# Sparse attention and FFN on one core: one written order for all engines, q and k ahead of the weights, and products of zeros at the beginning

## The chip, the cores and the metric

The kernel runs on one core of a Trainium2 chip. The metric is the time of one execution on the device in microseconds (us). A core has five engines that work side by side and wait for each other by semaphores: TensorE (PE in the profile; PEld is its weight load) multiplies matrices into PSUM; VectorE (DVE) and ScalarE (ACT) work element by element and can read PSUM; GpSimd (POOL) works element by element on SBUF; SyncE (SP) only issues transfers here. The kernels before and after are compared by the medians of their runs; the profile shows one execution.

## The reference

Eight batches, eight heads, 576 positions, heads of 64. Four heads look back over 32 positions, four at the positions of the same class modulo 32. The result, 4608 rows of 512, goes through a feed-forward layer with a gate that is 0 below -1, h above 1, and (h+1)^2/4 between.

```python
scores = scale * np.matmul(q, k.transpose(0, 1, 3, 2))
mask_local = (rel >= 0) & (rel < stride)
mask_strided = (rel >= 0) & (pos[None, :] % stride == pos[:, None] % stride)
...
scores = np.where(masks[None, :, :, :], scores, -1000000000.0)
scores = scores - np.max(scores, axis=-1, keepdims=True)
attn = np.exp(scores)
attn = attn / (np.sum(attn, axis=-1, keepdims=True) + 1e-09)
return np.matmul(attn, v).astype(np.float32)
...
x = np.ascontiguousarray(attn_out.transpose(0, 2, 1, 3)).reshape(B * S, H * D)
...
h = x @ w_in
g = np.where(pos, h, np.where(neg, 0.0, (h + beta) ** 2 / (4.0 * beta)))
return (g @ w_out).astype(np.float32)
```

## The kernel before, in words

**The feed-forward part.** The 4608 rows are cut into 12 chunks of 512, 384, 256 and then 384 rows. For each chunk c a loop runs over the 16 blocks f of 128 hidden units. `up(c, f)` makes the hidden block `hp` in PSUM with 12 products: four 128-wide pieces of x, each as three products of high and low parts (x and the weights are kept as two numbers each, so that the fast fp32r products are exact enough). The gate follows: ScalarE's Relu (L372) and Square (L373), VectorE's max and min (L374), then `gh`, the high part (L376 on ScalarE, L378 on VectorE in chunk 0), and `gl`, the low part (L379 on VectorE). `down(c, f)` adds three products for each 128 rows of the chunk into the output sums, 12 in chunk 0 and 9 in a chunk of 384. It runs two blocks behind `up` (`LAG = 2`). `hp` has two buffers in PSUM, so `up` of block f+2 waits until `gl` of block f has been read out.

**The weights.** Each f has 1 MB of float64 words (w_in's block and w_out's block side by side). They are loaded once, by SP, and turned to float32 pairs on the chip (`convert_w`): ScalarE's Prelu (L174) and Copy (L176) on the two words, VectorE's shift (L180), GpSimd's add (L181), then ScalarE's cast to the high part (L186) and VectorE's subtract for the low part (L188). One weight has two halves, so each step comes twice. Sixteen weights are converted: the first two tied in among batch 0's steps, the others up to three blocks ahead of their use (`AHEAD = 3`), during chunk 0. Several raw weights share buffers with converted ones or with q and k of batch 0 (`PLACES`), so their loads wait for those to be free.

**The attention part.** Each batch has four units: two of the local heads (12 and 6 blocks of 32 queries), two of the strided heads. Each unit goes through scores `s` (L261, TensorE), `soften` `e` (masks L283 and maximum L284 on VectorE, its subtraction on GpSimd L285, the exponent on ScalarE L287), `norm` `n` (sum L294, epsilon L295 and reciprocal L296 on VectorE, the multiplication on GpSimd L297), `flip` `f` (transposes L309 on TensorE, copies to SBUF L310 on ScalarE), values `v` (L326, TensorE) and `split` `x` (high part L342 on ScalarE, low part L343 on VectorE). Batch 0 runs before the loop. Batch b+1 runs inside a chunk that needs it next, its steps put between `up` and `down` of given blocks by the table `GROUPS`; batch 1 runs inside chunk 0.

**What sets the order.** TensorE's order is written out (`manual_schedule` for PE). On the other engines a planner with a model of the times orders the instructions, except those that are tied to program order (`pin`, `tie`): all of batch 0's, the loads, and the Prelu, Copy and shift of every weight. SP's loads come in this order: q and k of batch 0 (four transfers), w 0 whole, v (two), w 1 and 2, q and k of batch 1, w 3 to 5, the rest as buffers come free.

Of the kernel before, what the change touches and what calls it, by code (L numbers as in the profile page):

```python
# [8 lines left out]
F32 = mybir.dt.float32  # L9
# [14 lines left out]
def tile_sparse_attention_then_ffn(  # L24
# [42 lines left out]
    AHEAD = 3  # L67
    PRI = 1000
# [32 lines left out]
    make_identity(nc, ident)  # L101
    half = const.tile([P, 1], F32, name="half")
# [28 lines left out]
    wt, raws, held = {}, {}, set()  # L131
# [6 lines left out]
    def waits_in(f):  # L138
        return PLACES[f]

    pin = tc.keep_in_program_order

    def tie(ins, when):
        if when:
            pin(ins)

    def load_w(f):
        at = waits_in(f)
        held.add(at)
        if at < NF:  # L150
            raw = place(at, [P, 2, DM, 2], U32, f"raw_{f}")
            raws[f] = [(i, raw[:, i], slice(0, DM)) for i in range(2)]
            pin(nc.sync.dma_start(raw, w_v[f]))

    def pieces(f):
        if f in raws:
            yield from raws.pop(f)
            return
        n = DM // 2
        for i in range(2):  # L160
            for e in (slice(0, n), slice(n, DM)):
                r = o_p.tile([P, n, 2], U32, tag="ob", name=f"raw_{f}_{i}_{e.start}")
                pin(nc.sync.dma_start(r, w_v[f][:, i, e]))
                yield i, r, e

    def convert_w(f):

        held.discard(waits_in(f))
        parts = list(pieces(f))
        for _, raw, _ in parts:  # L170
            t = raw[:, :, 1].bitcast(F32)


            pin(nc.scalar.activation(t, t, AF.Prelu, scale=2.0 ** -112, alpha=2.0 ** 32))  # L174

            pin(nc.scalar.activation(raw[:, :, 0], raw[:, :, 0], AF.Copy, scale=2.0 ** -29))  # L176
        yield
        for _, raw, _ in parts:
            L, H_ = raw[:, :, 0], raw[:, :, 1]
            pin(nc.vector.tensor_scalar(out=H_, in0=H_, scalar1=3, scalar2=None, op0=ALU.logical_shift_left))  # L180
            tie(nc.gpsimd.tensor_tensor(out=H_, in0=H_, in1=L, op=ALU.add), f < 2)  # L181
        yield
        wt[f] = w = place(f, [P, 2, 2, DM], F32R, f"w_{f}")
        for i, raw, e in parts:
            t = raw[:, :, 1].bitcast(F32)
            tie(nc.scalar.copy(w[:, 0, i, e], t), f < 2)  # L186
            eng = nc.gpsimd if f == 0 else nc.vector
            tie(eng.tensor_tensor(out=w[:, 1, i, e], in0=t, in1=w[:, 0, i, e].bitcast(F32), op=ALU.subtract), f < 2)  # L188

    ready, staged, most = 0, 0, 6  # L190

    def stage(n):
        nonlocal staged
        while staged < min(NF, n) and waits_in(staged) not in held:
            load_w(staged)
            staged += 1

    def prepare(n):
        nonlocal ready
        while ready < min(NF, n):  # L200
            for _ in convert_w(ready):
                pass
            ready += 1
            stage(most)
# [4 lines left out]
    def load_qk(b, p):  # L209
        src = qk_l[b, p] if p < 2 else qk_s[b, p - 2]  # L210
        if b == 0 and p >= 2:
            t = place(NF + 1 - p, [P, 2, src.shape[2]], F32, f"qk_{b}_{p}")
        else:
            t = qk_p.tile([P, 2, src.shape[2]], F32, tag="qk", name=f"qk_{b}_{p}")
        load = nc.sync.dma_start(t, src)
        if b < 2:
            pin(load)
        loaded[b, p, "qk"] = t

    def load_v(b, p):  # L220
        src = (v_s if p else v_l)[b]
        t = v_p.tile(list(src.shape), F32, tag=f"v{p}", name=f"v_{b}_{p}")
        load = nc.sync.dma_start(t, src)
        if b < 2:
            pin(load)
# [16 lines left out]
    def attention(b, kinds):  # L242
# [4 lines left out]
        def score(u):  # L247
# [4 lines left out]
            for s in range(n):  # L252
                for p in range(2):
# [11 lines left out]
        def soften(u):  # L265

# [14 lines left out]
            for j in range(2):  # L281
                o = pr[:, j * n * 2:(j + 1) * n * 2].rearrange("p (n h) w -> p n h w", h=2)
                tie(nc.vector.tensor_tensor(out=o, in0=sc[j], in1=m, op=ALU.min), b == 0)  # L283
            tie(nc.vector.tensor_reduce(out=st[:, 0], in_=pr, axis=AX.X, op=ALU.max, negate=True), b == 0)  # L284
            tie(nc.gpsimd.tensor_tensor(out=pr, in0=pr, in1=st[:, 0].unsqueeze(2).broadcast_to([P, N, W]),  # L285
                                        op=ALU.add), b == 0)
            tie(nc.scalar.activation(pr, pr, AF.Exp, scale=scale), b == 0)  # L287
            probs[u] = room, st, n, W

        def norm(u):  # L290
            room, st, n, W = probs[u]
            N = 2 * n * 2
            pr = room[:, :N, :W]
            tie(nc.vector.tensor_reduce(out=st[:, 1], in_=pr, axis=AX.X, op=ALU.add), b == 0)  # L294
            tie(nc.vector.tensor_scalar(out=st[:, 2], in0=st[:, 1], scalar1=EPS, scalar2=None, op0=ALU.add), b == 0)  # L295
            tie(nc.vector.reciprocal(st[:, 2], st[:, 2]), b == 0)  # L296
            tie(nc.gpsimd.tensor_tensor(out=pr, in0=pr, in1=st[:, 2].unsqueeze(2).broadcast_to([P, N, W]),  # L297
                                        op=ALU.mult), b == 0)
            probs[u] = room, n

        def flip(u):

            room, n = probs.pop(u)
            pT = pt_p.tile([P, 2, SLOTS, P], F32, tag="pT", name=f"pT_{b}_{u}")
# [198 lines left out]
```

## Time and profile before

| | us |
|---|---|
| median of three runs | 943.62 (943.6 to 943.98) |
| the profiled execution: its time | 942.41 |
| the profiled execution: its span | 940.6 |
| TensorE busy in the span | 912.0 |
| first `up` product of chunk 0 starts at | 33.36 |
| first `up` product of chunk 1 starts at | 144.90 |
| last output product of chunk 11 ends at | 937.0 |

The profile has groups of rows. A row of the timeline gives the start from the beginning of the span, the duration, the engine, the line of the kernel, the operation, the tile written and the tiles read, and how many instructions are merged (x2); a bracket tells how long the engine stood idle just before and what ended that. A row of groups gives busy time, mean duration in ns of one instruction, and idle time before it. A row of waits gives who waited for whom: us in total, times, the longest. Products in TensorE overlap, so one of 0.39 us in a stream takes only the distance to the next one.

### The profile page before, as it was taken

Reading aid. Unit: us, or ns where it says so; the run is one execution under the profiler, and the core shown is the slowest. Engines: PE = TensorE matmul, PEld = TensorE weight load, DVE = VectorE, ACT = ScalarE, POOL = GpSimd, SP = SyncE. Lnnn points to the kernel's source line nnn. Section 1 sums busy time; section 2 is a strip of 40 time slices with the busy share of each in tenths; the row PEclk is TensorE's granted clock in tenths of the full one; section 3 lists DMA queues with packets and bytes.
Section 4 is the critical chain, followed back from the end, with each engine's and each line's share of the span. In section 5 each row is a group of like instructions: output and inputs, shape, how many; then the busy total and the mean of one; then the engine's idle time right before and its main releaser. Section 6 shows DMA issues by size and latency. Waiting matters only on the chain.

```text
span 940.6 us, 18900 instructions
## 1 busy us (share of the span) xinstructions
PE 912.0 (97%) x8112; PEld 800.4 (85%) x8112; DVE 383.9 (41%) x722; ACT 435.5 (46%) x859; POOL 129.4 (14%) x139
## 2 busy tenths in 40 slices
PE   4879999999999999999999999999999999999998
PEld 3657788898888889888888889898888888898987
DVE  6677863225444422234334433224433443222221
ACT  3677774334544444435444444334443443434433
POOL 6444430002102100002102100002110210000000
PEclk9989999999999999999999999999999999999999
DMA  9934411002311300002212211002021200000000
GB/s 377 363 122 154 160 44 45 0 1 88 103 55 54 102 32 34 1 1 88 102 32 87 57 48 63 1 1 87 16 88 33 86 1 1 34 1 1 34 1 34
DMA packets 14915, 61.95 MB, mean 66 GB/s; under 512 B 1648, under 2 KB 1648, under 8 KB 11888
## 3 DMA queue, kind: packets, MB, share of 16 engines
q1 hardware_dynamic: 14832, 60.76, 18.0%
q8 instruction: 63, 1.03, 0.5%
q14 instruction: 20, 0.16, 0.1%
HBM read 51.31 MB, written 9.44 MB: 65 GB/s over the span
## 4 chain that ended last, share of the span: by engine, by line
PE 88%; ACT 1%; DVE 1%; POOL 0%; issue 0%; DVEq 0%
PE o L388 42%; PE h L365 40%; PE xp L326 3%; PE sc L261 2%; PE tp L309 2%; ACT raw L174 0%; ACT raw L176 0%; DVE h L374 0%; DVE gh L378 0%; POOL pr L285 0%; DVE raw L180 0%; DVE gl L379 0%; ACT u L372 0%; DVE w L188 0%; ACT u L373 0%
## 5 line engine op out<-in xcount | busy, mean ns | idle before, releaser
L365 PE MATMUL h<-xTh,w 128*128 128x384 f32 (+2 forms) x1536 | 425.2, 339 | 9.3 <-ACT w L186 4.2
L388 PE MATMUL o<-w,gh 128*128 128x512 f32 x1152 | 369.7, 402 | 0.0
L365 PEld LDWEIGHTS h<-xTh,w 128*128 128x128 f32 x1536 | 280.9, 189 | 25.4 <-ACT w L186 4.7
L374 DVE SCALAR_TENSOR_TENSOR h<-h,u 128x384 f32<-128x384 f32 (+2 forms) x192 | 108.5, 565 | 403.9 <-ACT u L373 403.8
L365 PE MATMUL h<-xTl,w 128*128 128x384 f32 (+2 forms) x768 | 259.3, 338 | 0.0
L372 ACT ACTIVATE u<-h,half 128x384 f32<-128x384 f32 (+2 forms) x192 | 111.4, 580 | 318.5 <-PE h L365 316.7
L388 PEld LDWEIGHTS o<-w,gh 128*128 128x128 f32 x1152 | 208.3, 188 | 39.0
L388 PE MATMUL o<-w,gl 128*128 128x512 f32 x576 | 227.5, 395 | 0.0
L365 PEld LDWEIGHTS h<-xTl,w 128*128 128x128 f32 x768 | 145.5, 189 | 11.1
L379 DVE TENSOR_TENSOR gl<-h,gh 128x384 fp32r<-128x384 f32 (+2 forms) x192 | 106.5, 555 | 73.2 <-ACT gh L376 72.3
L388 PEld LDWEIGHTS o<-w,gl 128*128 128x128 f32 x576 | 107.9, 187 | 26.2
L376 ACT CAST gh<-h 128x384 fp32r<-128x384 f32 (+1 forms) x176 | 83.0, 472 | 88.0 <-DVE h L374 87.6
L285 POOL TENSOR_TENSOR pr<-pr,st 128x648 f32<-128x648 f32 (+2 forms) x32 | 41.3, 1291 | 519.7 <-DVE st L284 497.2
L373 ACT ACTIVATE u<-u 128x384 f32<-128x384 f32 (+2 forms) x192 | 101.2, 527 | 4.9
L287 ACT ACTIVATE pr<-pr 128x648 f32<-128x648 f32 (+2 forms) x32 | 23.7, 741 | 66.8 <-POOL pr L285 66.8
L297 POOL TENSOR_TENSOR pr<-pr,st 128x648 f32<-128x648 f32 (+2 forms) x32 | 40.8, 1275 | 42.7 <-DVE st L296 41.9
L294 DVE TENSOR_REDUCE st<-pr 128x12 f32<-128x648 f32 (+2 forms) x32 | 26.2, 818 | 44.2 <-ACT pr L287 44.2
L181 POOL TENSOR_TENSOR raw<-raw 128x512 uint32<-128x512 uint32 (+1 forms) x34 | 37.0, 1106 | 41.8 <-ACT u L373 14.7
L261 PEld LDWEIGHTS sc<-qk 64*32 64x32 f32 (+1 forms) x2048 | 28.2, 123 | 16.5 <-issue 8.0
L261 PE MATMUL sc<-qk 64*32 64x64 f32 (+1 forms) x2048 | 33.4, 234 | 8.7 <-DMA qk<-in_qk_l 5.4
L326 PEld LDWEIGHTS xp<-pT,v 64*64 64x64 f32 (+2 forms) x1856 | 33.0, 145 | 9.2 <-issue 5.7
L326 PE MATMUL xp<-pT,v 64*64 64x32 f32 (+2 forms) x1856 | 36.8, 230 | 1.3 <-ACT pT L310 1.3
(33 smaller groups left out, 368.6 us busy)
## 6 DMA issues: line engine op xcount, KB each, us to landing
raw<-in_w SPq DMA_DIRECT2D x15, 1024.0 KB, 10.1
qk<-in_qk_s SPq DMA_DIRECT2D x16, 604.0 KB, 5.3
qk<-in_qk_l SPq DMA_DIRECT2D x16, 576.0 KB, 4.8
v<-in_v_l SPq DMA_DIRECT2D x8, 1152.0 KB, 5.9
out<-ob SPq DMA_DIRECT2D x36, 256.0 KB, 4.1
v<-in_v_s SPq DMA_DIRECT2D x8, 704.0 KB, 4.2
raw<-in_w SPq DMA_DIRECT2D x4, 256.0 KB, 8.6
```

The costliest lines, as they stand in the source:

```text
L181: tie(nc.gpsimd.tensor_tensor(out=H_, in0=H_, in1=L, op=ALU.add), f < 2)
L261: nc.tensor.matmul(sc[j][i * Q:(i + 1) * Q, s, p], qk[:, 0, q0:q0 + Q], qk[:, 1, k0:k0 + W], start=True, stop=True)
L285: tie(nc.gpsimd.tensor_tensor(out=pr, in0=pr, in1=st[:, 0].unsqueeze(2).broadcast_to([P, N, W]), op=ALU.add), b == 0)
L297: tie(nc.gpsimd.tensor_tensor(out=pr, in0=pr, in1=st[:, 2].unsqueeze(2).broadcast_to([P, N, W]), op=ALU.mult), b == 0)
L326: nc.tensor.matmul(xp[p][j * D:(j + 1) * D, at:at + R], loaded[b, p0 // 2, "v"][half_, b0 + n, j], pT[half_, j, s, i * Q:i * Q + R], start ...
L365: nc.tensor.matmul(hp, wt[f][:, x, 0, cc * P:(cc + 1) * P], xT[y][:, cc, r0:r0 + n_t], start=n == 0, stop=n == 3 * NC - 1)
L372: nc.scalar.activation(u, hp, AF.Relu, bias=half, scale=0.5)
L373: nc.scalar.activation(u, u, AF.Square)
L374: nc.vector.scalar_tensor_tensor(out=hp, in0=hp, scalar=1.0, in1=u, op0=ALU.max, op1=ALU.min)
L376: nc.scalar.copy(gh, hp)
L379: nc.vector.tensor_tensor(out=gl, in0=hp, in1=gh.bitcast(F32), op=ALU.subtract)
L388: nc.tensor.matmul(o_ps[c][t], gs[x][:, t * P:(t + 1) * P], wt[f][:, y, 1, :], start=f == 0 and n == 0, stop=f == NF - 1 and n == 2)
```

## The change

It does five things.

1. Every engine runs in the order in which the program is written (`manual_schedule()` without a list of engines, over the whole kernel). The planner, the pins and `AHEAD` are gone. Steps that were one function are cut so that each engine's part can be placed: `soften` becomes mask `m`, below_max `a`, exponent `e`; `norm` becomes total `q`, plus_eps `p`, reciprocal and multiply `r`; `flip` keeps the transposes `f` and gets its copies as `c` (ScalarE) or `d` (VectorE); `split` becomes high `h` and low `l`.
2. Weights are loaded by halves. q and k of batch 0 come first; the load of the first half of w 0 waits for the third q,k transfer, by way of a copy of one number on ScalarE into the place the load will fill. Then v and the first halves of w 0 to 2 alternate.
3. The conversion is in five steps for each half (`conv_a` to `conv_e`). In chunk 0, `end_w` (cast and subtract) of given halves stands before a block's gate, `start_w` (Prelu and Copy, shift, add) of others after it. The first `up` is cut in two; its first four products use only the local heads' part of x.
4. Products of zeros on TensorE: 6 before the first scores, 12 after the last scores of batch 0.
5. Smaller ones: batch 1's steps in chunk 0 come two blocks later than other batches' (`S1` against `S0`); the epsilon moves from VectorE to ScalarE; the low part of w 0 from GpSimd to VectorE; the score products run over the pair of heads outside, over the slots inside; the copies of units 2 and 3 of batch 0 go to VectorE.

```diff
+    def load_w(f, i, after=None):
+        at = PLACES[f]
+        if i == 0:
+            held.add(at)
+            raws[f] = place(at, [P, 2, DM, 2], U32, f"raw_{f}")
+        if after is not None:
+            nc.scalar.copy(raws[f][0:1, i, 0:1, 0].bitcast(F32), after)
+        nc.sync.dma_start(raws[f][:, i], w_v[f][:, i])
...
+    def conv_a(f, i, low=(False, True)):
+        for raw, _ in pieces[f, i]:
+            t = raw[:, :, 1].bitcast(F32)
+            if False in low:
+                nc.scalar.activation(t, t, AF.Prelu, scale=2.0 ** -112, alpha=2.0 ** 32)
+            if True in low:
+                nc.scalar.activation(raw[:, :, 0], raw[:, :, 0], AF.Copy, scale=2.0 ** -29)
+    def conv_b(f, i):
...
+            nc.vector.tensor_scalar(out=H_, in0=H_, scalar1=3, scalar2=None, op0=ALU.logical_shift_left)
+    def conv_c(f, i):
...
+            nc.gpsimd.tensor_tensor(out=H_, in0=H_, in1=L, op=ALU.add)
+    def conv_d(f, i):
...
+            nc.scalar.copy(wt[f][:, 0, i, e], raw[:, :, 1].bitcast(F32))
+    def conv_e(f, i):
...
+            nc.vector.tensor_tensor(out=wt[f][:, 1, i, e], in0=raw[:, :, 1].bitcast(F32),
+                                    in1=wt[f][:, 0, i, e].bitcast(F32), op=ALU.subtract)
+    def start_w(*halves):
+        for f, i in halves:
+            conv_a(f, i)
+            conv_b(f, i)
+            conv_c(f, i)
+    def end_w(*halves):
+        for f, i in halves:
+            conv_d(f, i)
+            conv_e(f, i)
+        stage()
...
-            for s in range(n):
-                for p in range(2):
+            for p in range(2):
+                for s in range(n):
...
-            tie(nc.vector.tensor_scalar(out=st[:, 2], in0=st[:, 1], scalar1=EPS, scalar2=None, op0=ALU.add), b == 0)
+        def plus_eps(u):
+            nc.scalar.activation(st[:, 2], st[:, 1], AF.Copy, bias=EPS)
...
+    def gate(c, f, between=lambda: None):
+        n_t = CHUNKS[c]
+        hp = o_ps.pop((c, f))
...
         nc.scalar.activation(u, hp, AF.Relu, bias=half, scale=0.5)
         nc.scalar.activation(u, u, AF.Square)
+        between()
         nc.vector.scalar_tensor_tensor(out=hp, in0=hp, scalar=1.0, in1=u, op0=ALU.max, op1=ALU.min)
...
+    def warm(kind, n):
+        t = psum(kind, [P, P], f"warm_{kind}")
+        for _ in range(n):
+            nc.tensor.matmul(t, zeros, zeros, start=True, stop=True)
...
+    starts = {f: [] for f in range(NF)}
+    ends = {f: [] for f in range(NF)}
+    for g in range(1, NF):
+        if g > 1:
+            starts[g - 2].append((g, 0))
+        ends[g - 1].append((g, 0))
+    for g, at in enumerate((1, 2, 3, 4, 4, 5, 6, 6, 7, 7, 8, 9, 10, 11, 12, 14)):
+        starts[at].append((g, 1))
+        ends[at + 1].append((g, 1))
+    with tc.manual_schedule():
+        for p in range(4):
+            load_qk(0, p)
+        load_w(0, 0, loaded[0, 2, "qk"][0:1, 0, 0:1])
+        load_v(0, 0)
+        load_w(1, 0)
+        load_v(0, 1)
+        load_w(2, 0)
+        stage(6)
+        for p in range(2):
+            load_qk(1, p)
+        warm("o", 6)
+        first("s0 s1 s2 s3")
+        warm("o", 12)
+        first("m0 a0 m1 a1 e0 m2 a2 e1")
+        conv_a(0, 0, (False,))
+        first("q0 p0")
+        conv_a(0, 0, (True,))
+        first("e2 m3 r0 a3")
+        conv_a(1, 0)
+        first("q1 p1 r1 f0 c0 e3")
+        conv_b(0, 0)
+        conv_b(1, 0)
+        first("q2 p2 r2 v0 f1 q3 p3 r3")
+        conv_c(0, 0)
+        conv_c(1, 0)
+        first("f2 h0 l0 c1 d2 v1 h1 l1")
+        conv_d(0, 0)
+        first("v2 f3 d3 h2")
+        up(0, 0, last=False)
+        conv_e(0, 0)
+        first("l2 v3 h3 l3")
+        for p in range(2):
+            load_v(1, p)
+        up(0, 0, first=False)
...
+        S1 = {2: ("s0", "", "m0", "a0"), 3: ("s1", "e0 q0", "p0 m1", "a1 r0"), 4: ("", "e1 q1", "p1", "r1"),
+              5: ("f0", "", "c0", ""), 6: ("s2", "", "m2", "a2"), 7: ("v0", "e2 q2", "p2", "r2 h0 l0"),
+              8: ("f1", "", "c1", ""), 9: ("s3", "", "m3", "a3"), 10: ("v1", "e3 q3", "p3", "r3 h1 l1"),
+              11: ("f2", "", "c2", ""), 12: ("v2", "", "", "h2 l2"), 13: ("f3", "", "c3", ""),
+              14: ("v3", "", "", "h3 l3")}
...
             for f in range(NF):
+                if c or f:
+                    up(c, f)
+                pe, pre, mid, post = (S1 if c == 0 else S0).get(f, ("",) * 4) if b is not None else ("",) * 4
+                if pe:
+                    go(pe)
+                if c == 0:
+                    end_w(*ends[f])
...
+                if pre:
+                    go(pre)
+                pend.append((c, f, gate(c, f, lambda: mid and go(mid))))
+                if c == 0:
+                    start_w(*starts[f])
+                if post:
+                    go(post)
                 if len(pend) > LAG:
                     down(*pend.pop(0))
-                prepare(f + 1 + AHEAD)
```

`S0` is the same table with each entry two blocks earlier, except that f3 stands at 12 and v3 at 13.

More of the change, by code (lines that the diff above doesn't have):

```diff
@@ L193, in stage @@
+    staged = 0
+    def stage(n=NF - 1):
         nonlocal staged
-        while staged < min(NF, n) and waits_in(staged) not in held:
-            load_w(staged)
+        while staged < n and ((staged, 0) in pieces or PLACES[staged] not in held):
+            if (staged, 0) not in pieces:
+                load_w(staged, 0)
+            load_w(staged, 1)
             staged += 1
[L198 to L204, printed above, removed]
+    def start_w(*halves):
[3 more added lines that the diff above has]
+            conv_c(f, i)
@@ L263, in score, with mask @@
             probs[u] = sc, n, W
-        def soften(u):
+        def mask(u):
             local, b0, _ = UNITS[u]
```

192 lines of the change are left out of this document (79 added, 113 removed), and 4 rows, old and new, of the table S0.

## The prediction

> **What bounds the kernel now.** I read the page first: busy time, then the span in stretches.
>
> ```profile
> span 940.6 us, 18900 instructions
> PE 912.0 (97%) x8112; PEld 800.4 (85%) x8112; DVE 383.9 (41%) x722; ACT 435.5 (46%) x859; POOL 129.4 (14%) x139
> ```
>
> ```profile
> 10.00:20.00 10.00, 3.28 (x78) 2.90 (x70) 8.42 (x16) 5.34 (x9) 6.87 (x6) 1.00 1.01 420
> 30.00:40.00 10.00, 8.70 (x174) 6.95 (x167) 8.64 (x15) 9.48 (x19) 6.78 (x6) 1.00 0.87 292
> 150.00:200.00 50.00, 50.00 (x252) 45.05 (x252) 12.44 (x23) 20.30 (x39) 0.00 (x0) 1.00 0.06 22
> 900.00:940.60 40.60, 37.01 (x182) 32.50 (x180) 9.05 (x17) 14.46 (x27) 0.00 (x0) 1.00 0.05 20
> ```
>
> The columns of a stretch are busy us of TensorE, its weight loads, VectorE, ScalarE and GpSimd, then the granted clock, the DMA share and GB/s. TensorE idles 28.6 us (940.6 less 912.0): 3.6 at the end, 6.7 between 10 and 20 us, and with chunk 1 (150 us on) its column is full. Its own written order there does not change. Whatever the change is worth is decided before the first product of chunk 1. TensorE's longest wait on converted weights, and the marks of chunk 0 in the timeline (start, duration):
>
> ```profile
> PE h L365 <- ACT w L186: 4.2, 1, 4.2
> ...
> 37.09 0.39 PE L365 MATMUL h<-xTh,w 128*128 128x512 f32 x1
> ...
> 63.42 0.40 PE L365 MATMUL h<-xTh,w 128*128 128x512 f32 x1
> ...
> 141.88 0.39 PE L365 MATMUL h<-xTh,w 128*128 128x512 f32 x1
> ...
> 144.90 0.34 PE L365 MATMUL h<-xTh,w 128*128 128x384 f32 x1
> ```
>
> These are the last product of `up` for f=0 (ends 37.5), for f=3 (63.8), for f=15 (142.3), and chunk 1's first at 144.90. A round of chunk 0 costs (142.3 - 63.8) / 12 = 6.54 us, with the side engines in an order the planner chose; the first three cost 8.8 each, because the weights come late (4.2 us on L186) and the clock falls back.
>
> **Part 1, the beginning.** Loading q and k alone, weights by halves, normalisation interleaved unit by unit.
>
> ```profile
> 14.67 0.83 DVE L284 TENSOR_REDUCE st<-pr 128x12 f32<-128x648 f32 x1
> 18.81 2.56 PE L309 MATMUL tp<-ident,pr 128*128 128x128 f32 x10 [5.12 <-POOL pr L297]
> ```
>
> ```profile
> L310 ACT COPY pT<-tp 128x384 f32<-128x384 f32 x6 | 2.7, 491 | 4.8 <-PE xp L326 4.6 <-PE tp L309 0.2
> L342 ACT CAST xTh<-xp 128x252 fp32r<-128x252 f32 x2 | 1.2, 732 | 0.0
> L309 PEld LDWEIGHTS tp<-ident,pr 128*128 128x128 f32 x22 | 4.1, 220 | 6.7 <-POOL pr L297 6.6
> L326 PE MATMUL xp<-pT,v 64*64 64x32 f32 x144 | 4.3, 292 | 0.0
> L326 PE MATMUL xp<-pT,v 54*64 54x54 f32 x80 | 3.0, 313 | 1.3 <-ACT pT L310 1.3
> L326 PE MATMUL xp<-pT,v 36*64 36x36 f32 x8 | 0.6, 288 | 0.0
> ...
> L309 PEld LDWEIGHTS tp<-ident,pr 128*128 128x128 f32 x22 | 2.5, 141 | 1.0 <-issue 0.6 <-DVE xTl L343 0.2
> L326 PE MATMUL xp<-pT,v 64*64 64x32 f32 x144 | 2.5, 220 | 0.0
> L326 PE MATMUL xp<-pT,v 54*64 54x54 f32 x80 | 1.6, 222 | 0.0
> ```
>
> The groups above the dots are batch 0 (0 to 34 us), those below the same work of batch 1 (60 to 146 us). Transposes and the two wide kinds of values: 4.1 + 4.3 + 3.0 = 11.4 against 2.5 + 2.5 + 1.6 = 6.6 us.
>
> In the new order VectorE takes unit 3's masks and maximum before unit 0's reciprocal. By the row of before that maximum ends at 15.5; a reciprocal with its hand-overs (0.4, an estimate from the hand-overs of Part 2) and GpSimd's multiply of 128x768 (1.5, the add of that size in Part 2) put the first transpose at 17.4 instead of 18.81. Then TensorE's stream of transposes and values is the path. At batch 0's own price it takes 11.4, plus 0.6 for the last narrow blocks. Not covered are the evictions of unit 0's transposes on ScalarE (0.9, two copies of 0.49 that overlap a little) and of unit 3's on VectorE (1.0; its nearest row is the mask of the same width in Part 2, two in 1.01), unit 3's last split (one cast of 0.73 and two subtracts of about its length, 2.0), and the last eight products of `up` for f=0, which now wait for that split (8 x 0.23 = 1.8; it has four products done ahead by the split of `up`). 17.4 + 11.4 + 0.6 + 0.9 + 1.0 + 2.0 + 1.8 = 35.1 instead of 37.5: **2.4 us won**. Later bound 37.5, if the gated weight loads or the one-scalar copies that hold them, queued ahead of the exponents on ScalarE, eat the gain. On SP's queue the first half of w 0 now waits for the third q,k transfer, and v and all other halves stand behind it. At the 420 GB/s of the first stretch q, k, that half and v's local part (4.2 MB) are in by about 12 us with 2 us of start, and unit 0's values want v after 18; each further half of 512 KB takes 1.3 us, and the weights' adds stand behind unit 3's multiply on GpSimd anyway. So nothing is late by the loads.
>
> **The zero products** (6 and 12 of 128x128) sit in idle time of TensorE while it waits for loads and for GpSimd, so their own cost is nothing; 12 of them at 0.43 would last 5 us, from about 11.5 to 17, and without that cover would delay the first transpose by that much. What they can gain is the clock:
>
> ```profile
> 34.38 1.05 PE L365 MATMUL h<-xTh,w 128*128 128x512 f32 x2
> ...
> 81.43 0.62 PE L365 MATMUL h<-xTh,w 128*128 128x512 f32 x2
> ```
>
> A pair took 1.05 early and 0.62 later (0.43 and 0.23 apiece in a stream), while the granted clock shows 1.00 in the stretch of the early one. The slow price held after ten us of almost unbroken small products, so small products do not end it, and the zeros stop before the transposes start. I take the slow price; the fast one would save 11.4 - 6.6 = 4.8 us of Part 1.
> The Trainium skill, TensorE: Matmul & The Clock Gate, section "Part 1: The HAM clock gate", says that some 3.4 us of sustained products give full speed and an idle window of that length takes it away. By that rule the zeros would buy the 4.8 us, and the sum below would be 949.0 instead of 953.8; the rows above speak against "sustained" being met by the products that follow the zeros.
>
> **Part 2, chunk 0's written round.** This is the step that decides. In the new order each engine runs, per round f: ScalarE: casts of weight pieces begun in the round before, then Relu, Square, then Prelu and Copy of the next pieces. VectorE: subtracts for those casts, masks if any, L374, gh, gl, then the shifts of the next pieces. GpSimd: their adds, then attention's add or multiply. Relu(f+1) stands behind the casts, which wait for the adds, which wait for the shifts, which stand behind gl(f), which hangs on Relu(f). That is a closed loop, whatever TensorE does. Its hand-overs from the timeline:
>
> ```profile
> 87.19 0.69 ACT L186 CAST w<-raw 128x512 fp32r<-128x512 f32 x1 [0.78 <-POOL raw L181]
> 87.79 0.68 ACT L372 ACTIVATE u<-h,half 128x512 f32<-128x512 f32 x1
> ...
> 91.10 0.61 ACT L373 ACTIVATE u<-u 128x512 f32<-128x512 f32 x1
> 91.75 0.70 DVE L374 SCALAR_TENSOR_TENSOR h<-h,u 128x512 f32<-128x512 f32 x1 [3.14 <-ACT u L373]
> 92.55 0.69 DVE L378 CAST gh<-h 128x512 fp32r<-128x512 f32 x1
> 93.34 0.69 DVE L379 TENSOR_TENSOR gl<-h,gh 128x512 fp32r<-128x512 f32 x1
> 93.95 0.75 DVE L180 TENSOR_SCALAR raw<-raw 128x512 uint32<-128x512 uint32 x2
> 94.50 2.09 POOL L181 TENSOR_TENSOR raw<-raw 128x512 uint32<-128x512 uint32 x2 [7.21 <-ACT u L373]
> 95.63 0.68 ACT L186 CAST w<-raw 128x512 fp32r<-128x512 f32 x1 [1.74 <-POOL raw L181]
> ```
>
> Start to start: cast to Relu 0.60; Relu 0.71; Square to L374 0.65; to gh 0.80; to gl 0.79; to the shift 0.61; to the add 0.55; to the cast 1.13; and 1.05 for each further half. So a round costs 4.79 + 1.05 n for n halves. The lists `starts` put 30 halves in rounds 0 to 14 (mostly two, three in rounds 4, 6 and 7): 15 x 4.79 + 30 x 1.05 = **103.4 us** from Relu(0) to Relu(15), 6.9 a round against 6.54 now.
>
> On top come batch 1's attention steps that stand inside the loop:
>
> ```profile
> 42.22 1.01 DVE L283 TENSOR_TENSOR pr<-sc,m_loc 128x384 f32<-128x384 f32 x2
> ...
> 43.74 0.94 DVE L284 TENSOR_REDUCE st<-pr 128x12 f32<-128x768 f32 x1
> ...
> 44.83 1.47 POOL L285 TENSOR_TENSOR pr<-pr,st 128x768 f32<-128x768 f32 x1 [4.55 <-DVE st L284]
> ...
> 46.33 0.84 ACT L287 ACTIVATE pr<-pr 128x768 f32<-128x768 f32 x1 [2.58 <-POOL pr L285]
> ...
> 84.61 2.54 POOL L181 TENSOR_TENSOR raw<-raw 128x512 uint32<-128x512 uint32 x2 [2.88 <-ACT raw L176]
> 85.04 1.22 DVE L188 TENSOR_TENSOR w<-raw,w 128x512 fp32r<-128x512 f32 x1 [0.23 <-ACT w L186]
> ```
>
> Four times masks and maximum (1.01 + 0.94) stand ahead of L374; they start when the second cast's subtract is done (0.7 and 0.7 after the cast, so 0.8 after Relu starts) and end at 2.8, where L374 was due at 1.4; with the smaller units about 1.25 each, 4.9. Four times the exponent stands ahead of Relu and waits for GpSimd's add of the maximum, which is behind the weights' adds: 1.47 (1.05 to 1.3 in the smaller units), plus 0.73 of the exponent, less the 0.60 of a cast: 1.2 on average. And a subtract between two GpSimd instructions pushes the second back: the last two rows show 1.22 instead of 0.7, and GpSimd's pair 2.54 instead of 2.09. I count 0.69 at the four exponents and at two of the three third halves. Together 4.9 + 4.8 + 4.1 = **13.8**. Without the pushing it is 9.7, with every mask and exponent fitting into slack 0.
>
> After Relu(15), which comes as `up` f=15 ends, TensorE does one `down` (12 x 0.23 = 2.8) and reaches chunk 1: 35.1 + 103.4 + 13.8 + 2.8 = **155.1** against 144.90. TensorE's own products fit into such a round (at most 6.54 by its marks), so it waits instead of setting the pace.
>
> **Part 3, the rest of the kernel.** From chunk 1 on no weights are converted, so the loop is open. Written order puts a mask ahead of L374 there as well; 1.95 of it lies beside TensorE's `down`, `up`, `down` (some 30 products of at least 0.17, 5.1 us) before `up(f+2)` needs the PSUM buffer, against 3.6 for Relu to gl. The full column of 150 to 200 us stays full. I take 0; with that cover gone it is at most 2 us for each mask. The swapped loops of the score products, the sum's epsilon on ScalarE and the copies of two units' transposes on VectorE change no count that TensorE waits for after batch 0.
>
> **Sum.** The profiled execution took 942.41 us (span 940.6 and 1.8 around it). 942.41 + 155.1 - 144.9 = 952.6. The median of the runs, 943.62, is 1.2 above that execution; carried over, 953.8.
>
> **Rivals.** *The loop does not close* (faster): if the casts find their adds done, because hand-overs overlap more than the rows say, chunk 0 keeps 6.54 a round: 35.1 + 98.1 + 2.8 = 136.0, 8.9 less than now, 934.7; halfway, the bare loop with all extras hidden, 35.1 + 103.4 + 2.8 = 141.3, gives 940.0. For it: ScalarE and VectorE are not full (46 and 41%). Against it: order, not load, makes the loop. It decides once the mean round, extras included, falls under (144.9 - 35.1 - 2.8) / 15 = 7.13; I get 7.81. *The clock falls back* (slower still): the loop leaves TensorE waits of 3 to 5 us in rounds 1 to 5, and after the 4.2 us on L186 the products ran at 0.43:
>
> ```profile
> 61.17 1.05 PE L365 MATMUL h<-xTh,w 128*128 128x512 f32 x2
> ```
>
> 24 products a round then cost 10.3 instead of 5.5, more than the loop: half of four rounds at 4.8 exposed gives 10 us, 963. *The beginning wins nothing*: 37.5, so 2.4 more, 956. *The zeros keep the clock up*: 4.8 less, 949. *The order is not as written*, the planner still moves things: no change, 943.6.
>
> **How the numbers follow.** Forecast 953.8, chance 0.50, its own range 947 to 960; clock 0.12; beginning 0.06; zeros 0.10; all slower. The faster rival 0.18; unchanged order or a draw 0.04. Within 0.2% means within 1.9 us of 943.62, about what a measurement can tell. Faster 0.18, same 0.04, slower 0.78. The range reaches to the bare loop below and the clock's case above: 939 to 963.
>
> **What would show it.** The first `up` ends near 35 and chunk 1's first product starts near 155 (right) or before 145 (wrong). In chunk 0, Relu starts 6.9 us apart or more, ScalarE's waits ahead of its casts are put down to GpSimd's weight adds, and TensorE's waits name the casts or subtracts of weights. After chunk 1's first product both traces must run alike. A mean Relu pace under 7.1 would make the prediction wrong, and so would TensorE idling under 20 us before 150.

## The result, and the profile after

The changed kernel takes 948.87 us, the median of four runs (947.9 to 951.77), beside 943.68 for the kernel before in the same sitting: 1.006 times the time, 95% interval 1.0038 to 1.0081. It is slower by 5.2 us. Slower was forecast, but by 10.2: 953.8. The profiled execution took 947.9 (span 946.1).

The head of the page, the stretch of 30 to 150 us (columns as in the prediction) and the first product of chunk 1:

```profile
span 946.1 us, 19016 instructions
PE 918.8 (97%) x8148; PEld 805.7 (85%) x8148; DVE 387.6 (41%) x697; ACT 443.3 (47%) x888; POOL 126.8 (13%) x137
...
30.00:150.00 120.00, 102.89 (x865) 79.93 (x865) 88.16 (x138) 82.49 (x152) 46.35 (x42) 0.93 0.42 151
...
150.36 0.34 PE L398 MATMUL h<-xTh,w 128*128 128x384 f32 x1
```

Chunk 1 starts at 150.36 instead of 144.90, 5.5 later. What follows takes 946.1 - 150.36 = 795.7 us, as in the kernel before (940.6 - 144.90 = 795.7). So everything happened ahead of chunk 1. From 30 to 150 us TensorE idles 17.1 us; the same stretch of the kernel before:

```profile
30.00:150.00 120.00, 108.39 (x956) 85.56 (x949) 93.79 (x154) 85.02 (x158) 48.94 (x44) 0.96 0.39 143
```

There it idles 11.6. The page alone would mislead here: TensorE's idle time over the whole span fell, from 28.6 to 27.3 us, because its busy time now holds the zeros. The starts of Relu in chunk 0, of the kernel before and after (count, shortest/median/longest ns, first and last start):

```profile
L372 ACT ACTIVATE u<-h,half x16: 669/688/734, 39.4 to 142.3; 128x512 f32<-128x512 f32 x16
```

```profile
L408 ACT ACTIVATE u<-h,half x16: 669/677/707, 32.4 to 149.9; 128x512 f32<-128x512 f32 x16
```

The change comes to its first Relu 7 us earlier and to its last one 7.6 later: (149.90 - 32.35) / 15 = 7.84 us a round instead of 6.86. An ordinary round of the changed kernel (timeline, one engine after the other):

```profile
122.43 0.68 ACT L408 ACTIVATE u<-h,half 128x512 f32<-128x512 f32 x1
123.14 0.63 ACT L409 ACTIVATE u<-u 128x512 f32<-128x512 f32 x1
...
127.89 0.67 ACT L181 CAST w<-raw 128x512 fp32r<-128x512 f32 x1 [1.12 <-POOL raw L175]
128.89 0.67 ACT L181 CAST w<-raw 128x512 fp32r<-128x512 f32 x1 [0.33 <-POOL raw L175]
129.46 0.68 ACT L408 ACTIVATE u<-h,half 128x512 f32<-128x512 f32 x1
...
123.98 0.69 DVE L411 SCALAR_TENSOR_TENSOR h<-h,u 128x512 f32<-128x512 f32 x1
124.77 0.69 DVE L415 CAST gh<-h 128x512 fp32r<-128x512 f32 x1
125.56 0.69 DVE L416 TENSOR_TENSOR gl<-h,gh 128x512 fp32r<-128x512 f32 x1
126.17 0.76 DVE L170 TENSOR_SCALAR raw<-raw 128x512 uint32<-128x512 uint32 x2
...
126.82 2.04 POOL L175 TENSOR_TENSOR raw<-raw 128x512 uint32<-128x512 uint32 x2 [3.32 <-ACT raw L165]
```

The loop can be walked: Relu 122.43, Square, L411, gh, gl, the shifts at 126.17, the adds at 126.82, the casts at 127.89 and 128.89, Relu again at 129.46. Nothing in it waits for TensorE. ScalarE had finished its own work of the round (Prelu, Copy) by 126.8 and stood idle ahead of both casts. GpSimd stood idle for 3.3 us and then was what everybody waited for. Its bracket names ScalarE's Copy (L165), because that ended at 126.8 as well; what it had to have was the shift: in the round before, the Copies were done at 119.2 and the adds still came at 119.78, 0.65 after the shifts at 119.13, just as here. Waits of 30 to 155 us (us in total, times, longest):

```profile
POOL raw L175 <- DVE raw L170: 48.6, 9, 10.2
ACT w L181 <- POOL raw L175: 27.1, 28, 2.8
```

GpSimd waits for VectorE's shifts, and ScalarE's casts wait for GpSimd. In the kernel before, the wait of the casts for the adds, over 30 to 150 us, is a third of that:

```profile
ACT w L186 <- POOL raw L181: 9.2, 13, 1.8
```

### The profile page after: what moved, and what is told of

It is laid out like the page before. It is cut to its first block, busy times and chain, and to the rows that moved or that the text cites. A ratio compares the mean times of both kernels' runs of the same rounds, so it can differ in the third digit from the quotient of the medians.

```text
span 946.1 us, 19016 instructions
## 1 busy us (share of the span) xinstructions
PE 918.8 (97%) x8148; PEld 805.7 (85%) x8148; DVE 387.6 (41%) x697; ACT 443.3 (47%) x888; POOL 126.8 (13%) x137
## 3 DMA queue, kind: packets, MB, share of 16 engines
q8 instruction: 64, 1.05, 0.4%
## 4 chain that ended last, share of the span: by engine, by line
PE 87%; DVE 2%; DMA 1%; ACT 1%; POOL 0%; issue 0%; SPq 0%; DVEq 0%; POOLq 0%
PE o L425 41%; PE h L398 39%; PE xp L345 3%; PE sc L263 2%; PE tp L318 2%; DMA raw<-in_w 1%; DVE raw L170 1%; DVE w L185 0%; POOL raw L175 0%; ACT w L181 0%; DVE xTl L369 0%; DVE gh L415 0%; DVE h L411 0%; ACT raw L165 0%; ACT raw L162 0%
## 5 line engine op out<-in xcount | busy, mean ns | idle before, releaser
L425 PE MATMUL o<-w,gh 128*128 128x512 f32 x1152 | 374.9, 406 | 5.8 <-ACT w L181 3.1
L411 DVE SCALAR_TENSOR_TENSOR h<-h,u 128x384 f32<-128x384 f32 (+2 forms) x192 | 108.5, 565 | 348.7 <-ACT u L409 348.5
L425 PEld LDWEIGHTS o<-w,gh 128*128 128x128 f32 x1152 | 210.8, 190 | 47.4 <-DVE w L185 4.0
L425 PE MATMUL o<-w,gl 128*128 128x512 f32 x576 | 229.8, 399 | 0.0
L290 POOL TENSOR_TENSOR pr<-pr,st 128x648 f32<-128x648 f32 (+2 forms) x32 | 42.3, 1324 | 482.9 <-DVE st L285 442.4
L307 POOL TENSOR_TENSOR pr<-pr,st 128x648 f32<-128x648 f32 (+2 forms) x32 | 42.4, 1326 | 72.9 <-DVE st L306 48.9
L175 POOL TENSOR_TENSOR raw<-raw 128x512 uint32<-128x512 uint32 (+1 forms) x34 | 34.7, 1040 | 76.8 <-DVE raw L170 48.6
L185 DVE TENSOR_TENSOR w<-raw,w 128x512 fp32r<-128x512 f32 (+1 forms) x34 | 31.4, 930 | 19.3 <-ACT w L181 19.3
L345 PEld LDWEIGHTS xp<-pT,v 64*64 64x64 f32 (+2 forms) x1856 | 30.3, 134 | 9.6 <-issue 4.2
L345 PE MATMUL xp<-pT,v 64*64 64x32 f32 (+2 forms) x1856 | 34.3, 221 | 1.5 <-ACT pT L326 1.0
```

Source lines behind the costliest of these rows:

```text
L345: nc.tensor.matmul(xp[p][j * D:(j + 1) * D, at:at + R], loaded[b, p0 // 2, "v"][half_, b0 + n, j], pT[half_, j, s, i * Q:i * Q + R], start ...
L411: nc.vector.scalar_tensor_tensor(out=hp, in0=hp, scalar=1.0, in1=u, op0=ALU.max, op1=ALU.min)
L425: nc.tensor.matmul(o_ps[c][t], gs[x][:, t * P:(t + 1) * P], wt[f][:, y, 1, :], start=f == 0 and n == 0, stop=f == NF - 1 and n == 2)
```

## The experiments

The rival theories. **Closed loop**: ScalarE, VectorE and GpSimd set chunk 0's rounds, because a round's pieces are started behind its gate and finished ahead of the next one. **TensorE**: its products, slowed by a clock that falls back, set them. Ratios are against the kernel before on the same chip, with 95% intervals.

**1. The pieces started ahead of the gate.** The same instructions, one place earlier, in rounds 0 to 13.

```diff
+                if c == 0 and f < NF - 2:
+                    start_w(*starts[f])
                 if pre:
                     go(pre)
                 pend.append((c, f, gate(c, f, lambda: mid and go(mid))))
-                if c == 0:
+                if c == 0 and f >= NF - 2:
                     start_w(*starts[f])
```

> One line moved: in rounds 0 to 13 of chunk 0 the Prelu, Copy, shift and add of the next weight halves stand ahead of the gate instead of behind it. Theory of the closed round (Relu waits for casts, these for GpSimd's adds, these for shifts that stood behind gl of the round before): the round opens, Relu runs at about TensorE's own 6.3 us in place of 7.8, chunk 1's first product starts near 126 to 130 us instead of 150.4, the time is 924 to 929. Rival, the side engines are simply full in chunk 0, or the clock sets the pace: order does not matter, 945 to 950. Rival, the shifts now delay L374 by as much as they save: 943 to 948.

928.44 us, ratio 0.9842 (0.9825 to 0.9858): faster than both kernels, by 14 us than the one before on the same chip. The rounds' stretch, Relu, and waits of 30 to 135 us:

```profile
36.00:131.00 95.00, 92.30 (x858) 73.36 (x857) 77.27 (x135) 79.70 (x149) 42.85 (x42) 1.00 0.48 172
...
L408 ACT ACTIVATE u<-h,half x16: 665/687/742, 36.2 to 130.5; 128x512 f32<-128x512 f32 x16
...
ACT u L408 <- PE h L398: 9.8, 7, 3.5
...
ACT w L181 <- POOL raw L175: 2.5, 7, 0.6
```

The casts' wait for the adds fell from 27.1 to 2.5 us, and Relu now waits for TensorE (9.8 us). A round takes (130.5 - 36.2) / 15 = 6.29. Same counts, same engines: it was the order. Chunk 1's first product comes at 131.44, a little later than the 126 to 130 expected. The granted clock is 1.00 in these rounds, beside 0.93 in the changed kernel from 30 to 150 us, so this experiment by itself does not part the order from the clock; the round walked above, in which nothing waits for TensorE, and experiment 3, which gives TensorE no more work, do. This execution even came to its first Relu 3.9 us later than the changed kernel.

**2. Batch 1's masks, maxima, exponents, sums and epsilons of chunk 0 behind the gate**, with the loop left closed.

```diff
                 pe, pre, mid, post = (S1 if c == 0 else S0).get(f, ("",) * 4) if b is not None else ("",) * 4
+                if c == 0 and ("m" in mid or "p" in mid):
+                    pre, mid, post = "", "", f"{pre} {mid} {post}"
```

> In chunk 0 the masks, maximum, exponent, sum and epsilon of batch 1 stand behind the gate and the weight steps instead of ahead of L374 and of Relu; everything else as after. Closed round with 13.8 us of attention extras (4.9 masks, 4.8 exponents, 4.1 pushing): between 9 and 12 us of them go, chunk 1 starts near 139 to 141 us, the time is 937 to 940, and Relu runs at 6.9 us a round. Rival, the extras lie in slack and the weights alone set the pace: 947 to 950.

940.77 us, 0.9978 (0.9969 to 0.9987). The first Relu starts at 33.2, the last at 141.5:

```profile
L408 ACT ACTIVATE u<-h,half x16: 675/686/699, 33.2 to 141.5; 128x512 f32<-128x512 f32 x16
```

A round takes 7.22. Batch 1's steps in the loop, the extras of the prediction, are worth about 8 us by the medians, a little less than the 9 to 12 expected; without them the closed loop is near the time of the kernel before, not at that of the open loop.

**3 and 4. A second add on GpSimd** behind each weight add of f=2 to 15, in the closed and in the open loop. Its result is read by nobody.

```diff
             nc.gpsimd.tensor_tensor(out=H_, in0=H_, in1=L, op=ALU.add)
+            if f > 1:
+                nc.gpsimd.tensor_tensor(out=L, in0=L, in1=L, op=ALU.add)
```

> The changed kernel with a second add on GpSimd behind each weight add of f=2 to 15 (low part plus itself, read by nobody): 28 halves, about 1.05 us each. If the closed loop over ScalarE, VectorE and GpSimd sets chunk 0's rounds, every one of them lands on the path: 28 x 1.05 = 29 us more, 974 to 982, and Relu starts about 9.7 us apart. Rival, TensorE or its clock sets the rounds: GpSimd has idle time in every round (it is busy 8.7 us in the 20 us from 80 on less than VectorE), so at most 4 more, 949 to 953.

> The same second add in the kernel whose pieces are started ahead of the gate in rounds 0 to 13. The adds now have a whole round before the casts that want them (GpSimd then has about 4.2 us of weights in a round of 6.3, with attention's steps 7 in some). Open loop: only what stands behind the adds in the rounds with an exponent shows, up to 4 x 2.1, so 929 to 938 (e_open took 928.4). If GpSimd's own speed is the cause and not the order: 28 x 1.05 = 29 more here too, 955 to 960.

Closed: 973.38 us, 1.0321 (1.0305 to 1.0336). Open: 938.38, 0.995 (0.9931 to 0.9969). Against the same kernels without the second add that is 24.5 and 9.9 us for the same 28 halves of weights, so their place decides, and most of their time lands on the path only where the loop is closed. The closed one stayed just under its range: 0.88 us for each half instead of 1.05. The open one ended just above its own. The casts' wait in the closed one, 33 to 174 us:

```profile
ACT w L183 <- POOL raw L175: 49.6, 29, 2.8
```

27.1 us became 49.6: 22.5 more, and chunk 1's first product came at 174.02 instead of 150.36.

**5. Both cures at once**: the edits of 1 and 2.

> Pieces started ahead of the gate and batch 1's masks, maxima, exponents, sums and epsilons of chunk 0 behind it, both at once. In the closed loop the second alone was worth 8 us. If with the loop open TensorE sets the rounds, these steps lie beside it: no further gain, 926 to 930. If ScalarE's and VectorE's order ahead of the gate still delays Relu: 4 to 8 less than 928.4, 920 to 924.

936.28 us, 0.9927 (0.991 to 0.9943), 8 slower than the open loop alone: outside both ranges. One wait points at the reason:

```profile
ACT st L302 <- DVE st L298: 13.4, 4, 4.8
```

In experiment 1 that wait is 0.8 us. With the whole softmax in one place, the sum stands on VectorE behind the weights' subtracts and shifts and behind the gate, and ScalarE waits for it with its epsilon, ahead of the casts. That this wait makes all of the 8 us was not tested by itself. A step that helps a closed order can slow an open one.

**6. The beginning as written, the chunks' other engines ordered by the planner.**

```diff
+    with tc.manual_schedule(engines={mybir.EngineType.PE}):
         S0 = {0: ("s0", "", "m0", "a0"), ...
```

> Batch 0 in written order as after; from chunk 0's loop on only TensorE is written and the planner orders the other engines, as it did before. If the written order of the loop alone costs what was lost: rounds of about 6.5 us as before from a first Relu at 32.35, chunk 1 near 132 us, the time 929 to 934. If the planner without the ties of before orders the loop no better: 943 to 955.

956.77 us, 1.0151 (1.0136 to 1.0166), above both of its ranges. The stretch ahead of the rounds, and Relu:

```profile
40.00:60.00 20.00, 10.28 (x67) 7.32 (x65) 20.00 (x30) 17.91 (x32) 10.36 (x10) 0.59 0.68 260
...
L408 ACT ACTIVATE u<-h,half x16: 667/687/707, 62.0 to 156.8; 128x512 f32<-128x512 f32 x16
```

The planner filled VectorE (20.00 of 20), mostly with shifts and subtracts of weights, among which batch 0's last copies and splits had to wait, so that the first Relu came at 62.0 instead of 32.4. Its rounds then took 6.32. This does not undo one part cleanly, since the beginning changed with it and the pieces were converted early; it shows that rounds of 6.3 are to be had with these products.

**7 to 9. The zero products.** The changed kernel without them; the kernel before with them, at the same two places; the open loop without them.

```diff
-        warm("o", 6)
         first("s0 s1 s2 s3")
-        warm("o", 12)
```

> After without the 18 products of zeros. If they keep TensorE's clock up for batch 0: transposes and values go back to the price of before (11.4 instead of about 7 us), the first Relu starts 3 to 5 us later than 32.35, chunk 1 as much later, the time is 951.5 to 954. Rival, batch 0 is fast for another reason or the zeros only fill time: 947.5 to 949.5.

> The kernel before with the 18 zero products at the same two places of TensorE's order (6 ahead of the scores, 12 behind them), nothing else changed. If they buy speed for the transposes and values of batch 0 by themselves: 2 to 4.8 less, 938.5 to 941.5. If they need the new order of the beginning, or if the 2.7 us seen without them was one execution's clock: 942.5 to 944.

> The kernel with pieces started ahead of the gate, without the 18 zero products. If they are worth about the same in every order (2 to 3 us by the two pairs so far): 930.4 to 931.5. If in this order, where the profiled execution ran its first 30 us at a granted clock of 0.58 to 0.83 in spite of them, they buy nothing: 927.5 to 929.5.

950.43 us (1.0085, 1.0069 to 1.01), 940.06 (0.9972, 0.9962 to 0.9981) and 928.64 (0.9842, 0.9829 to 0.9856). By the medians the zeros are worth 1.6 us in the changed kernel (2.4 by the ratios, whose intervals overlap: 1.0038 to 1.0081 with them), between the two ranges expected; 3.2 in the kernel before (2.6 by the ratio); and nothing in the open loop. Between nothing and 3 us, then, and not the full 4.8 anywhere. (In the rows each product of zeros is two records.) The kernel before with them shows how they wear off, and below the dots the open loop with them (experiment 1):

```profile
18.96 0.88 PE L311 MATMUL tp<-ident,pr 128*128 128x128 f32 x6 [1.11 <-POOL pr L299]
...
22.12 0.87 PE L311 MATMUL tp<-ident,pr 128*128 128x128 f32 x6 [1.05 <-POOL pr L299]
22.93 2.78 PE L328 MATMUL xp<-pT,v 64*64 64x32 f32 x96
25.64 1.54 PE L311 MATMUL tp<-ident,pr 128*128 128x128 f32 x6
...
20.77 2.77 PE L345 MATMUL xp<-pT,v 64*64 64x32 f32 x96 [3.44 <-ACT pT L326]
```

The six transposes take 0.88 and 0.87, and 1.54 again 3.5 us later. In the open loop the values come 4.4 us after the last zeros and are slow at once (2.77): in that execution the zeros had worn off before the values began. In the profile of the changed kernel without zeros (experiment 7) the first Relu came 2.2 us later than with them, but a transfer was late there too (the next experiments), so that profile does not isolate the clock.

**10. The first half of the weights of f=0 not held back** until the third q,k transfer is in.

```diff
-        load_w(0, 0, loaded[0, 2, "qk"][0:1, 0, 0:1])
+        load_w(0, 0)
```

> The changed kernel without the one-element copy that holds the first half of the weights of f=0 until the third q,k transfer is in. The prediction took the hold at nothing. If it is nothing: 947.5 to 950.5, as the changed kernel (948.9). Rival, the hold brings q and k in earlier: that half is 512 KB and shares the queues with them, 1.3 us at the 420 GB/s of the first stretch, so 950 to 951. Other rival, the copy itself delays ScalarE or the weights behind it: 1 to 2.4 less, 946.5 to 948.

949.62 us, 1.0071 (1.0058 to 1.0085). The difference to the changed kernel is within the intervals: the hold is worth nothing that shows.

**11 and 12. ScalarE's work on the first half of f=1 behind unit 0's transposes**, in the closed and in the open loop. The profiles of the beginning show unit 0's copies (L326) behind a Prelu (L162) that waits for its transfer; in the open loop of experiment 1:

```profile
19.06 0.65 ACT L162 ACTIVATE raw<-raw 128x512 f32<-128x512 f32 x1 [4.29 <-DMA raw<-in_w]
...
20.26 0.84 ACT L326 COPY pT<-tp 128x384 f32<-128x384 f32 x2
```

```diff
-        conv_a(1, 0)
         first("q1 p1 r1 f0 c0 e3")
+        conv_a(1, 0)
```

> The changed kernel with ScalarE's Prelu and Copy of the first half of the weights of f=1 moved behind unit 0's transposes and the copies of them (and unit 3's exponent). In the profiles so far that Prelu starts when its transfer is in, at 15.9 to 19.8 us, and unit 0's copies stand behind it. If the transfer holds the beginning: the values of unit 0 start within 0.9 us of the end of unit 0's transposes, 0.9 to 2 us earlier in all, 946.5 to 948.2. Rival, GpSimd's multiplies or the clock bind next at once: 948.5 to 949.5.

> The same move in the kernel whose pieces are started ahead of the gate, where the values of unit 0 waited 3.4 us for those copies in its profile. If the transfer holds the beginning there: Relu of f=0 starts 2 to 3.4 us earlier than 36.2 and the time falls to 925 to 927. If another wait takes its place: 928 to 929.

Closed: 948.95 us, 1.0066 (1.0053 to 1.008), nothing. Open: **926.0**, 0.982 (0.9806 to 0.9833), the fastest of all; its runs lie at 925.43 to 926.09, those of experiment 1 at 926.49 to 929.17, though the intervals of the ratios still touch. In the closed one the values start at 18.35 instead of 19.06, after a wait for v, and the next transposes wait for GpSimd:

```profile
18.35 1.60 PE L345 MATMUL xp<-pT,v 64*64 64x32 f32 x96 [1.47 <-DMA v<-in_v_l]
...
23.13 0.87 PE L318 MATMUL tp<-ident,pr 128*128 128x128 f32 x6 [2.59 <-POOL pr L307]
```

In the open one the first Relu starts at 32.4 instead of 36.2:

```profile
L408 ACT ACTIVATE u<-h,half x16: 663/687/705, 32.4 to 126.6; 128x512 f32<-128x512 f32 x16
```

## Why the prediction was right, point by point

**What bounds the kernel: right.** The time is decided ahead of chunk 1; what follows is the same to 0.1 us.

**Part 1, the beginning: right in sign, too small.** 2.4 us were forecast and 35.1 for the first Relu; it starts at 32.35, 2.7 earlier still. The rows of the changed kernel:

```profile
12.17 5.28 PE L436 MATMUL warm_o<-zeros 128*128 128x128 f32 x24
17.29 0.82 PE L318 MATMUL tp<-ident,pr 128*128 128x128 f32 x6
19.06 1.98 PE L345 MATMUL xp<-pT,v 64*64 64x32 f32 x96 [0.95 <-ACT pT L326]
...
23.00 0.88 PE L318 MATMUL tp<-ident,pr 128*128 128x128 f32 x6 [1.38 <-POOL pr L307]
...
14.57 1.47 POOL L307 TENSOR_TENSOR pr<-pr,st 128x768 f32<-128x768 f32 x1 [1.25 <-DVE st L306]
...
17.34 0.68 ACT L162 ACTIVATE raw<-raw 128x512 f32<-128x512 f32 x1 [2.65 <-DMA raw<-in_w]
...
18.55 0.84 ACT L326 COPY pT<-tp 128x384 f32<-128x384 f32 x2
```

The mis-sized term is TensorE's stream of 11.4: six transposes at 0.82 instead of 1.54, 96 values at 1.98 instead of 2.79. The whole stream is 8.3 us by its rows (8.6 with a gap of 0.35 among them), where the sum has 11.4 + 0.6 = 12.0. The wait of 1.38 for GpSimd's multiply, which the sum does not have, took part of that back. The first transpose at 17.4 was met (17.29), but for another reason: GpSimd's multiply ended at 16.0, 1.3 before, and TensorE was still busy with zeros. So the zeros were not free, as the prediction had it; they held unit 0's transposes up by about a microsecond, which the copies behind the late Prelu hid. "Nothing is late by the loads" was wrong as well: ScalarE waited 2.65 us for that half. Experiments 11 and 12 show its price: nothing in this kernel, where GpSimd's multiply and the closed loop stand next, and 2.4 us by the medians once the loop is open. The zeros, the hold and the place of that Prelu were tried one by one; the other edits of the beginning were not, so how the earlier Relu divides among them stays open.

**The zero products: value taken too low.** I took the slow price, gain nothing; experiments 7 to 9 put it between nothing and 3 us, by what stands around. The rule of the Trainium skill that the prediction quotes (TensorE: Matmul & The Clock Gate, "Part 1: The HAM clock gate") gave 949.0 and so came within 0.2 of the time, but in part by luck: batch 0's stream did run at the fast price in the changed kernel, as that sum has it, yet 4.8 us is more than the zeros brought in any pair, and the loop below was over-priced. On its idle window, some 3.4 us, this case leaves the rule open. In experiment 8 no idle stretch between the zeros and the slow values was longer than 1.11 us; but from the end of the zeros (17.85) to the values (22.93) TensorE ran nothing except transposes, 5.1 us. If transposes do not count, the rule fits; no run here tests that by itself. The step "small products do not end it" was wrong as a general statement: without zeros (experiment 7) the same small products began slow and became fast within one profile, with no wider product ahead of them (columns as in the prediction):

```profile
21.54 3.16 PE L345 MATMUL xp<-pT,v 64*64 64x32 f32 x96 [3.62 <-ACT pT L326]
...
26.96 1.66 PE L345 MATMUL xp<-pT,v 64*64 64x32 f32 x96
...
20.00:30.00 10.00, 8.46 (x212) 7.60 (x212) 7.18 (x15) 6.29 (x17) 5.61 (x5) 1.00 1.02 412
```

So a part of the fast price of the changed kernel would have come without the zeros too.

**Part 2, the closed round: right, and a little dear.** From the first Relu to the fifteenth, 14 rounds with 29 halves: 14 x 4.79 + 29 x 1.05 = 97.5 by the bare formula, and 109.6 measured:

```profile
32.35 0.69 ACT L408 ACTIVATE u<-h,half 128x512 f32<-128x512 f32 x1 [1.97 <-PE h L398]
...
141.92 0.68 ACT L408 ACTIVATE u<-h,half 128x512 f32<-128x512 f32 x1
...
147.69 0.44 ACT L162 ACTIVATE raw<-raw 128x256 f32<-128x256 f32 x1 [3.79 <-DMA raw<-in_w]
```

The round shown above took 7.03, where the formula has 6.89. The extras were 12.1 instead of 13.8. The four rounds with a mask and an exponent took 10.02, 9.10, 11.14 and 9.52, together 39.8 beside 28.6 by the formula (three with two halves, one with three): 11.2 of the 12.1. In the dearest, from Relu at 79.22 to 90.36 with three halves (7.94 by the formula):

```profile
79.98 0.89 DVE L284 TENSOR_TENSOR pr<-sc,m_str 128x324 f32<-128x324 f32 x2
80.91 0.83 DVE L285 TENSOR_REDUCE st<-pr 128x12 f32<-128x648 f32 x1
81.65 0.69 DVE L411 SCALAR_TENSOR_TENSOR h<-h,u 128x512 f32<-128x512 f32 x1
...
88.72 1.51 DVE L185 TENSOR_TENSOR w<-raw,w 128x512 fp32r<-128x512 f32 x1 [0.18 <-ACT w L181]
...
87.95 1.73 POOL L290 TENSOR_TENSOR pr<-pr,st 128x648 f32<-128x648 f32 x1
...
89.71 0.75 ACT L294 ACTIVATE pr<-pr 128x648 f32<-128x648 f32 x1 [1.02 <-POOL pr L290]
90.36 0.67 ACT L408 ACTIVATE u<-h,half 128x512 f32<-128x512 f32 x1
```

Mask and maximum put L411 at 2.4 after Relu instead of 1.4; the add of the maximum waits for three weight adds, the exponent for it, Relu for the exponent; and a subtract beside GpSimd takes 1.51. All three mechanisms are there. By the same rows of all four rounds, masks and maxima cost 4.4 instead of 4.9 (L411 behind Relu, less the 1.36 of the formula), and the exponents with their pushed adds 6.9, where 4.8 and 2.8 of the pushing were counted (Relu behind the last cast, less 0.60). What is left is 0.8, where the third halves had 1.4. So each of the three was taken a little too high. The 1.7 between 13.8 and 12.1 is part of the 4.7 by which chunk 1 started earlier than 155.1; 2.7 come from Part 1. That the order makes the loop, which the prediction only argued, experiments 1, 3 and 4 show.

The last Relu (149.9) was held by a weight piece's transfer (the row at 147.69, 3.79 us), but TensorE did not wait for it: chunk 1's first product comes 8.4 after the fifteenth Relu, where the prediction has 8.6.

**Part 3: right**, 0.

**The rivals.** *The loop does not close* falls by the 27.1 us of waits; experiment 1 reaches its pace, 6.29 instead of 6.54, and betters its 934.7, but by another order. *The beginning wins nothing* falls by the first Relu at 32.4. *The clock falls back*: it did, but not at the forecast price. The granted clock from 30 to 150 us is 0.93, beside 0.96 before, and pairs of products took 1.06 again:

```profile
39.15 1.06 PE L398 MATMUL h<-xTh,w 128*128 128x512 f32 x2
```

The ten rounds among the 14 without mask and exponent sum to 0.9 us above the formula, so TensorE's slow stretches lie beside the loop. No run held the clock up in this kernel's rounds, so their price by itself stays open. *The order is not as written* falls by the round shown.

**The markers.** Chunk 1's first product was to come near 155 or, to refute it, before 145; 150.36 lies between, and the 4.7 by which it misses 155.1 is accounted for above. Relu starts under 7.1 apart were to refute it; the mean is 7.84. That this is so near the 7.81 forecast is partly luck: the last round took 7.98 instead of 5.84 because of that transfer. The casts' waits are put down to GpSimd's adds, as forecast. TensorE's waits of 30 to 150 us name casts and subtracts of weights for 9.0 us; another 7.8, in three waits, stand ahead of attention's transposes, which the prediction did not have. TensorE's idle time before 150 us was a poor marker: 23.7 us (the 17.1 from 30 on and 6.6 before), above the 20 that I set, but the kernel before has 25.0 there.

## What to carry to other kernels

In an order written for several in-order engines, walk once round each cycle of hand-overs: an operand finished ahead of a step and started behind the step before it makes a loop whose length is the sum of its hand-overs, however idle the engines are. Start such work one step earlier before moving anything else, and look at each moved step for what then stands behind it; the same move won 8 us in one order and lost 8 in the other. A wait for a load in a written order holds all that stands behind it on that engine, so place it by when the data is in, not by when the engine is free. Products that are to bring TensorE to the fast price pay only if real products follow them closely (next section).

## What the runs showed of the hardware

At the beginning of an execution a granted clock of 1.00 does not tell which price small products pay. From 20 to 30 us it is 1.00 in the kernel before, where 96 values took 2.79, and 1.00 in experiment 7, where 96 took 3.16 and then 1.66 (fence above). Behind the zeros it does follow the price: from 20 to 30 us it is 1.00 in the changed kernel (96 values in 1.98), 0.65 in the kernel before with zeros (2.78) and 0.58 in experiment 1 (2.77).

How long the fast price lasts behind the zeros can be read from the ten profiles in which the first transposes after them were fast (0.82 to 0.88). Take the stretches in which TensorE ran only transposes or nothing. After stretches of up to 2.8 us the values were still fast (1.60 to 1.98 for 96; experiments 2, 3, 10, the changed kernel, and the first stretch of 11 and of 12). After 4.4 us and more they were slow in all four (experiments 1, 4, 5 and 8: 2.77 to 3.15). In between, 3.5 us brought the slow price back in experiment 12 (2.67) and 4.0 us did not in experiment 11 (2.04). These are readings of single profiles; no run changed that stretch alone.

The time at which one transfer among many lands varies by more than most edits of the beginning are worth. The Prelu that waits for the first half of f=1 began at 17.34 us in the changed kernel, at 19.06 in experiment 1, where nothing that precedes it differs, and at 15.93 without the hold. The stretch of 10 to 20 us moved 318 GB/s in experiment 1, 378 in the changed kernel and 406 without the hold.
